# First stage of batches 3 to 7 from input folded twice, in rounds of sixteen 24x24 tiles; the last batch's evictions mostly on ScalarE

## The chip, the cores and the metric

The kernel runs on one core of one Trainium2 chip. The metric is the device time of one execution in microseconds; the figure that counts is the median of the runs shown. The engines go by their short names in the profile: PE is TensorE (its weight loads are PEld), DVE is VectorE, ACT is ScalarE, POOL is GpSimd and SP is SyncE.

## What is computed

The input x has 8 batches of 3008 positions with 256 channels. Each batch is filtered along its positions in the frequency domain, and the result goes through a two-layer network with an exact GELU:

```python
X = np.fft.rfft(x, axis=1)
y = np.fft.irfft(X * (filt_r + 1j * filt_i)[None], n=x.shape[1], axis=1)
h = y.reshape(24064, 256) @ w_in            # 256 -> 2048
g = 0.5 * h * (1.0 + erf(h / sqrt(2)))
out = g @ w_out                             # 2048 -> 256, float32
```

## The kernel before, in words

**The transform as four stages of matmuls.** 3008 = 47 x 64. A batch is seen as 47 rows (n1) of 64 positions (h = 0 or 1, w = 0 to 31). Stage one (`s1`) is a transform of length 47 over n1. Because x is real, the output is needed for 24 frequencies only (K1 = 24), a cosine and a sine part each. Before it `fold` (L104) forms sum and difference of the halves h = 0 and h = 1 in bf16 on DVE (L109, L110): four calls c a batch, each of 4 values of w in two groups v, 111 partitions x 1024 elements. `s1` (L414, matmuls on L429) then issues eight matmuls in a call: 47 rows of x against a table of 64 columns, 512 columns wide, into four PSUM banks (one of tag "h", three of tag "f"). Two banks are emptied by DVE (L327) and two by ACT (L325), and SP writes the result to a DRAM buffer R1 (L438). `r1` (L444, SP) reads R1 back as `b_sb`, in three parts u. `s2` (L456) is stage two, 32 small matmuls a burst; `s2_out` (L467, DVE) multiplies by the filter, `s2_sum` (L473, L474, DVE) adds up complex products, `s3` (L487) is stage three, `s3_out` writes to a DRAM buffer R2 (L497, SP), `r2` (L505, SP) reads it as `d_sb`, and `s4` (L514) is stage four, evicted into a ring `y_sb` of two batches of positions. Batch 0 goes another way (`c1` to `c4`) in the first 41 us.

**The network.** The 24064 positions form 47 token tiles t of 512. `mm1` (L640) makes 16 blocks jc of h in PSUM (tag "h", 3 banks), and ACT applies GELU (L643) into `g_sb`. The second layer of tile t-1 runs while tile t goes through the first. From t = 3 on it is `mm2_seven` (L698): seven products of half-size blocks take the place of eight, 112 matmuls of 128 columns (L714), with sums on DVE before (`sums_1` L685, `sums_2` L691, `sums_3` L696) and after (L729 to L743). Product m has matmuls 16m to 16m+15. They go through two PSUM banks of tag "o": product 0 in one, 1 and 2 in the other, 3 and 4 in the first, 5 and 6 in the second. Product 2 reads what `sums_2` writes, its second half (matmul 36 on) what the second L691 writes. L743 empties product 6, and `put_rows` (L761) writes the output rows, mostly from POOL.

**Order.** Every engine runs its instructions in the order in which they are recorded, and that order is laid out by hand in slots. A slot is one jc of one tile (slot = 16t + jc, about 0.83 us): whatever is put in the slot, then seven matmuls of `mm2_seven`, then one block of `mm1`. Batch b's stages are put in slots counted back from hi, the slot in which its first token tile begins (L918 to L945). Bursts of `s1` for batches 3 to 6 stand at hi-94, -91, -87 and -83, for batch 7 four slots earlier, and folds 20, 13, 8 and 6 slots ahead of hi-94. The x buffer is single: `load_next` (L144) loads the next batch's x in the slots of this batch's stage two, each time behind a small `gate` instruction on POOL that waits for a product of that stage. `table_4_factors` (L389) and `table_4_all` (L402, POOL) make the table of stage four in slots 46, 47, 89 and 105.

Of the kernel before, what the change touches and what calls it, by code (L numbers as in the profile page):

```python
# [18 lines left out]
NA, NB = 47, 64  # L19
# [12 lines left out]
class _Mix:  # L32
    def __init__(self, ctx, tc, x, filt_r, filt_i, w_in, w_out, out):
# [30 lines left out]
        self.s4_sb = f[:, 0:2048].bitcast(FP16).rearrange("p (i n) -> p i n", i=8)  # L64
        self.v_sb = [f[:, o:o + 1024].rearrange("p (c d) -> p c d", c=2) for o in (2048, 3072)]
        self.T4a = f[0:96, 4096:7168].rearrange("p (w m) -> p w m", w=HB)
        self.w_in_sb = c.tile([128, 2, self.DFF], BF16, name="w_in_sb")
# [15 lines left out]
    def load_x(self, lo=0, n=32, hs=(0, 1)):  # L83
        nc = self.nc
        if lo == 0 and 0 in hs:
            xt = self.px.tile([128, HB, 256], BF16, tag="x", name="x_sb")
            self.st[0, "x"], self.st["x1"] = xt[0:2 * NA], xt.rearrange("p (h w) c -> p h w c", h=2)
        xt, o = self.st[0, "x"], NA
        xv = self.x[0].rearrange("(n1 h w) d -> h n1 w d", h=2, w=HB)
        for w in range(lo, lo + n, 8):  # L90
            for h in hs:
                nc.gpsimd.dma_start(out=xt[h * o:h * o + NA, w:w + 8, :], in_=xv[h][:, w:w + 8, :])  # L92

    def load_x_pairs(self, b, c, h, n=1):
# [3 lines left out]
        for v in range(2):  # L98
            for to, at, m in ((0, 23, 24), (24, 0, 23)) if h else ((0, 0, NA),):
                w = 16 * v + 4 * c  # L100
                self.nc.gpsimd.dma_start(out=xt[64 * v + to:64 * v + to + m, h, 4 * c:4 * c + 4 * n, :],  # L101
                                         in_=xv[h][at:at + m, w:w + 4 * n, :])

    def fold(self, b, c):  # L104
# [39 lines left out]
    def load_next(self, b, p, c, h):  # L144
# [3 lines left out]
        else:  # L148
            self.gate(self.st[b, "p", p][0:1, p % 2, 1, 0, 0:1])
        self.load_x_pairs(b + 1, c, h)  # L150

# [180 lines left out]
    def table_1_tiles(self, g):  # L332
# [4 lines left out]
        for p in (0, 64):  # L337
            for r in (0, K1):
                v.tensor_copy(out=self.T1s[p:p + NA, r:r + K1].rearrange("p (u c m) -> p u c m", c=4, m=2),
                              in_=self.T1[0:NA, r:r + K1].rearrange("p (c u m) -> p u c m", u=3, m=2))  # L340

    def table_2_parities(self):

# [156 lines left out]
    def r2(self, b, c):  # L500
        d = self.pd.tile([96, 8, 256], BF16, tag="d", name="d_sb")
        self.st[b, "d", c] = d
        R2 = self.st[b, "R2"].rearrange("(r w) u a k m c -> r (u a k m) w c", r=2)
        for r in range(2):
            self.nc.sync.dma_start(out=d[r * 48:r * 48 + 48, :, :], in_=R2[r][:, 8 * c:8 * c + 8, :])  # L505

# [191 lines left out]
    def mm2_seven(self, t, lo, hi):  # L698
# [9 lines left out]
        for n in range(lo, hi):  # L708
# [32 lines left out]
            else:  # L741
                for h, tt, p in ((1, t3, p0), (0, t1, p1)):
                    v(out=c(h, 1 - h), in0=tt, in1=p, op=ALU.add)  # L743
                    for sub in range(2):
                        self.put_rows(t * TCH + 256 * h + 128 * sub, self.st["c"][h][:, sub],
                                      nc.gpsimd if t > 1 or h * sub == 0 else nc.sync)

# [35 lines left out]
def kernel(  # L783
# [135 lines left out]
    for b in range(1, B):  # L919
# [5 lines left out]
        for c in range(4):  # L925
            slot = (4, 8, 11, 13)[c] if b == 1 else s1 + int(c * n1)
            put((0, 1, 5, 8)[c] if b == 1 else (70, 74, 86, 94)[c] if b == 2 else hi - 94 - (20, 13, 8, 6)[c], m.fold, b, c)
            put(slot, m.s1, b, c)
# [11 lines left out]
        after[b] = s3 + 4  # L940
        crowd.update(range(s2[0], after[b]), range(s1 + 66, s1 + 94))
        if b + 1 < B:
            for i, (u, o, p) in enumerate(((0, 5, 1), (0, 7, 1), (1, 1, 2), (1, 5, 3), (1, 7, 3), (2, 1, 4), (2, 5, 5), (2, 7, 5))):
# [29 lines left out]
    put(9, m.table_4_rows, g)  # L973
    put(9, m.weights_4, g)
    put(23, m.table_u)
    put(46, m.table_4_factors, g)
    parts = [(w, h) for w in range(0, HB, 8) for h in range(2)]
    put(47, m.table_4_all, parts[:5])
    for slot, i, n in ((89, 5, 2), (105, 7, 1)):
        put(slot, lambda: m.gate(m.s4_sb[0:1, 7, 255:256]))  # L980
        put(slot, m.table_4_all, parts[i:i + n])
# [58 lines left out]
```

## Time and profile before

| | us |
|---|---|
| median of the 3 runs | 733.25 (733.07 to 733.67) |
| the profiled execution | 733.37 |
| its span in the profile | 731.6 |
| PE busy, all first-stage matmuls (L429) of 7 batches in the chain | 2.1% of the span |
| DVE busy | 595.1 |
| ACT busy | 576.6 |
| POOL busy | 283.9 |

The profile shows one execution. Its span goes from the first to the last instruction; the execution's own time is 1.77 us longer. Matmuls are pipelined, so their ends are modelled and a busy PE can still have waited: distances between starts tell more. "Idle before" of a group counts only what its own engine stood still. The engines' shares, by stretch of the span (busy us and instructions of each engine, granted clock, DMA share, GB/s), are even from batch 3 on:

```profile
core 0: us, PE busy (x) PEld busy (x) DVE busy (x) ACT busy (x) POOL busy (x), PEclk, DMA share, GB/s
...
354.00:443.00 89.00, 88.97 (x1195) 64.42 (x1193) 75.74 (x138) 71.89 (x132) 32.65 (x63) 1.00 0.50 125
443.00:532.00 89.00, 88.95 (x1155) 60.95 (x1153) 76.00 (x139) 71.84 (x132) 33.29 (x66) 1.00 0.51 126
532.00:621.00 89.00, 89.00 (x1218) 62.96 (x1216) 77.31 (x143) 73.05 (x136) 18.99 (x34) 1.00 0.42 118
```

Each of these stretches holds about one batch: 89 us, PE busy throughout at the full clock (1.00), DVE 76 us, ACT 72 us, and the 16 DMA engines half busy.

### The profile page before, as it was taken

How to read it: one execution, taken by the hardware profiler on the slowest of the kernel's cores; microseconds unless marked ns; L12 is line 12 of the kernel's file. 1: busy time of each engine (PE TensorE's matmuls, PEld its weight loads, DVE VectorE, ACT ScalarE, POOL GpSimd, SP SyncE). 2: the span in 40 equal slices, each digit the busy share in tenths (PEclk: the TensorE clock that was granted, in tenths of full speed). 3: DMA queues.
4: the chain of work that ended last, by engine and by line, in shares of the span. 5: the costliest groups of instructions: out<-in, count | busy, mean ns of one | idle time of the engine just before them, and what ended most of it. 6: DMA issues, size and time to landing. Idle time of an engine off the chain costs nothing.

```text
span 731.6 us, 22218 instructions
## 1 busy us (share of the span) xinstructions
PE 722.6 (99%) x9165; PEld 505.9 (69%) x9165; DVE 595.1 (81%) x1091; ACT 576.6 (79%) x1050; POOL 283.9 (39%) x545
## 2 busy tenths in 40 slices
PE   7999999999999999999999999999999999999997
PEld 4856675776777666676777667666677767777776
DVE  8985788899878998798976999779988897775666
ACT  7997778788877888778887788877888788877773
POOL 7944947364223462135511364115531121121121
PEclk9999999999999999999999999999999999999999
DMA  9886545664365553636535455355545443311011
GB/s 155 163 182 152 132 107 123 205 127 98 88 179 135 119 115 107 183 92 137 128 109 157 120 129 126 87 149 151 110 102 138 139 119 87 109 46 43 30 59 59
DMA packets 81254, 87.72 MB, mean 120 GB/s; under 512 B 13393, under 2 KB 61137, under 8 KB 81153
## 3 DMA queue, kind: packets, MB, share of 16 engines
q0 software_dynamic: 22288, 39.50, 24.1%
q1 hardware_dynamic: 58449, 46.62, 23.6%
q8 instruction: 71, 1.16, 0.7%
q14 instruction: 30, 0.25, 0.1%
q10 hardware_dynamic: 416, 0.20, 0.1%
HBM read 54.00 MB, written 46.66 MB: 138 GB/s over the span
## 4 chain that ended last, share of the span: by engine, by line
PE 94%; ACT 3%; DVE 1%; POOL 1%; DMA 1%; issue 0%; ACTq 0%; DVEq 0%; POOLq 0%
PE ps_h L640 44%; PE ps_o L714 38%; PE ps_o L656 3%; PE ps_s L514 3%; PE ps_s L429 2%; PE ps_s L456 2%; PE ps_s L487 2%; DMA F<-in_filt_i_dram 1%; ACT y_sb L325 1%; POOL x_sb L92 1%; ACT g_sb L643 1%; ACT vt_sb L325 0%; ACT b_sb L325 0%; PE ps_c L587 0%; DVE p L474 0%
## 5 line engine op out<-in xcount | busy, mean ns | idle before, releaser
L643 ACT ACTIVATE g_sb<-ps_h 128x512 f16<-128x512 f32 x752 | 446.3, 601 | 139.1 <-PE ps_h L640 130.4
L640 PE MATMUL ps_h<-y_sb,w_in_sb 128*128 128x512 bf16 (+3 forms) x1600 | 446.0, 366 | 0.3 <-ACT g_sb L643 0.3
L761 POOL DMA_DIRECT2D out_dram<-ost x231 | 131.8, 577 | 379.4 <-DVE ost L743 366.1
L714 PEld LDWEIGHTS <-g_sb 128*128 128x128 f16 x2816 | 184.4, 98 | 80.8 <-issue 14.6
L640 PEld LDWEIGHTS <-w_in_sb 128*128 128x128 bf16 x1600 | 126.2, 98 | 7.6 <-issue 1.6
L714 PE MATMUL ps_o<-w_sums,g_sb 128*128 128x128 f16 x1408 | 121.7, 219 | 0.3 <-DVE g_sb L691 0.2
L714 PE MATMUL ps_o<-w_sums,s_sb 128*128 128x128 f16 x1408 | 121.2, 219 | 0.0
L714 PEld LDWEIGHTS <-s_sb 128*128 128x128 f16 x1408 | 95.1, 98 | 37.6 <-issue 2.5
L685 DVE TENSOR_TENSOR s_sb<-g_sb 128x1024 f16<-128x1024 f16 x176 | 115.2, 685 | 0.7 <-ACT g_sb L643 0.6
L714 PE MATMUL ps_o<-w_out_sb,g_sb 128*128 128x128 f16 x1408 | 113.7, 219 | 0.0
L467 DVE TENSOR_TENSOR p<-ps_s,Fu 128x1024 bf16<-128x1024 f32 x84 | 101.5, 1217 | 9.1 <-PE ps_s L456 7.5
L101 POOL DMA_DIRECT2D x_sb<-in_x_dram x156 | 79.5, 516 | 2.8 <-issue 1.7
L691 DVE TENSOR_TENSOR g_sb<-s_sb,g_sb 128x1024 f16<-128x1024 f16 x88 | 60.4, 687 | 1.5
L714 PE MATMUL ps_o<-w_out_sb,F 128*128 128x128 f16 x704 | 60.6, 219 | 0.0
L696 DVE TENSOR_TENSOR F<-g_sb 128x1024 f16<-128x1024 f16 x88 | 60.0, 682 | 0.0
L714 PEld LDWEIGHTS <-F 128*128 128x128 f16 x704 | 47.1, 98 | 14.6 <-issue 0.4
L736 DVE TENSOR_TENSOR t_sb<-t_sb,ps_o 128x256 f32<-128x256 f32 x44 | 18.4, 417 | 40.4 <-PE ps_o L714 39.9
L514 PEld LDWEIGHTS <-d_sb 96*128 96x128 bf16 x448 | 31.3, 97 | 27.0 <-issue 1.7
L325 ACT ACTIVATE F<-ps_s 128x512 bf16<-128x512 f32 x83 | 45.5, 607 | 0.5 <-PE ps_s L487 0.4
L325 ACT ACTIVATE y_sb<-ps_s 128x376 bf16<-128x376 f32 x95 | 45.4, 478 | 0.1
L327 DVE CAST a_sb<-ps_s 128x512 bf16<-128x512 f32 x54 | 34.7, 684 | 12.0 <-PE ps_s L429 11.7
L743 DVE TENSOR_TENSOR ost<-t_sb,ps_o 128x256 f32<-128x256 f32 x86 | 32.1, 414 | 14.2 <-PE ps_o L714 14.2
(160 smaller groups left out, 588.7 us busy)
## 6 DMA issues: line engine op xcount, KB each, us to landing
out_dram<-ost POOLq DMA_DIRECT2D x127, 128.0 KB, 2.9
b_sb<-R SPq DMA_DIRECT2D x21, 512.0 KB, 4.9
R<-F SPq DMA_DIRECT2D x84, 128.0 KB, 2.4
d_sb<-R SPq DMA_DIRECT2D x56, 192.0 KB, 4.3
R<-a_sb SPq DMA_DIRECT2D x108, 96.0 KB, 2.2
x_sb<-in_x_dram POOLq DMA_DIRECT2D x48, 94.0 KB, 2.7
x_sb<-in_x_dram POOLq DMA_DIRECT2D x48, 48.0 KB, 2.7
x_sb<-in_x_dram POOLq DMA_DIRECT2D x12, 188.0 KB, 4.7
```

The source lines that it names most:

```text
L101: self.nc.gpsimd.dma_start(out=xt[64 * v + to:64 * v + to + m, h, 4 * c:4 * c + 4 * n, :], in_=xv[h][at:at + m, w:w + 4 * n, :])
L325: self.nc.scalar.activation(out=out, in_=in_, func=AF.Copy, scale=1.0 if scale is None else scale)
L327: self.nc.vector.tensor_copy(out=out, in_=in_)
L467: v(out=w[:, a], in0=ps.unsqueeze(2).to_broadcast([128, 2, 2, 256]), in1=f.unsqueeze(1).to_broadcast([128, 2, 2, 256]), op=ALU.mult)
L514: nc.tensor.matmul(ps[:, 94 * i:94 * i + 94], lhsT=d[:, (grp % 2) * 4 + i, 128 * half:128 * half + 128], rhs=self.T4a[:, 4 * grp + i, 0:2 ...
L640: nc.tensor.matmul(ps[:, o:o + n], lhsT=w[:, dc], rhs=self.ring[:, dc, off:off + n], start=(dc == 0), stop=(dc == 1))
L643: nc.scalar.activation(out=self.st["g", t][:, jc, :], in_=ps, func=AF.Gelu)
L685: self.nc.vector.tensor_tensor(out=self.st["s", t][:, i:i + 2], in0=a, in1=b, op=ALU.subtract)
L691: self.nc.vector.tensor_tensor(out=a21[:, k], in0=self.st["s", t][:, k, 0], in1=a22[:, k], op=ALU.add)
L696: self.nc.vector.tensor_tensor(out=self.s4_sb[:, k], in0=a12[:, k], in1=s2[:, k], op=ALU.subtract)
L714: nc.tensor.matmul(ps[:, (m + 1) % 2, sub, :], lhsT=a[:, i, 128 * sub:128 * sub + 128], rhs=b[:, i], start=i == 0, stop=i == 7)
L761: eng.dma_start(out=out, in_=tile_[lo - r0:lo - r0 + n])
```

## The change

For batches 3 to 7 the input is folded a second time. A cosine is even and a sine odd in n1, so rows n1 and 47-n1 can be added and subtracted ahead of stage one. That leaves 24 rows instead of 47 for each part. For this the rows 24 to 46 have to stand on the partitions of rows 23 to 1. `turn_x` (three POOL DMAs a batch, from DRAM to DRAM) writes the mirrored half of x as bf16 into a DRAM buffer xr, 12 slots ahead of the previous batch's stage two. `load_x_mirror` then loads the direct half from x (POOL) and the mirrored half from xr (SP), eight times each. `fold_mirror` runs eight DVE operations a batch on 120 partitions x 2048 elements: for each half k of w two from x into a scratch area in the F tile, then two back into x. Each stage-one call (`s1_mirror`) issues 16 matmuls of 24 rows x 32 columns, 512 columns wide, on 16 different tiles of the array (four row groups, each with a PSUM bank of its own, times four column groups). In batches 3 to 6 two of the four banks are emptied by DVE and two by ACT as before, in batch 7 one by DVE and three by ACT. The table T1m for it is made on POOL in slot 9.

Besides this, `table_4_factors` moves from slot 46 to 33 and five parts of `table_4_all` from slot 47 to slots 34, 51 and 53; the first `r2` of batch 6 is split in two halves of w; and the output rows of the last three tiles are written from SP instead of POOL.

```diff
@@ -63,6 +63,7 @@
         f = self.F.rearrange("p t k c -> p (t k c)")
         self.s4_sb = f[:, 0:2048].bitcast(FP16).rearrange("p (i n) -> p i n", i=8)
         self.v_sb = [f[:, o:o + 1024].rearrange("p (c d) -> p c d", c=2) for o in (2048, 3072)]
+        self.fold_t = f[:, 8192:12288].rearrange("p (d e w c) -> p d e w c", d=2, e=2, w=4)
         self.T4a = f[0:96, 4096:7168].rearrange("p (w m) -> p w m", w=HB)
         self.w_in_sb = c.tile([128, 2, self.DFF], BF16, name="w_in_sb")
         self.w_out_sb = c.tile([128, 16, self.D], FP16, name="w_out_sb")
@@ -84,7 +85,9 @@
         nc = self.nc
         if lo == 0 and 0 in hs:
             xt = self.px.tile([128, HB, 256], BF16, tag="x", name="x_sb")
+            self.px_x = xt
             self.st[0, "x"], self.st["x1"] = xt[0:2 * NA], xt.rearrange("p (h w) c -> p h w c", h=2)
+            self.st["xm"] = xt.rearrange("p (h e w) c -> p h e w c", h=2, e=2)
         xt, o = self.st[0, "x"], NA
         xv = self.x[0].rearrange("(n1 h w) d -> h n1 w d", h=2, w=HB)
         for w in range(lo, lo + n, 8):
@@ -100,6 +103,52 @@
                 w = 16 * v + 4 * c
                 self.nc.gpsimd.dma_start(out=xt[64 * v + to:64 * v + to + m, h, 4 * c:4 * c + 4 * n, :],
                                          in_=xv[h][at:at + m, w:w + 4 * n, :])
+
+    def turn_x(self, b):
+
+        D, n = self.D, NB * self.D
+        xr = self.st["xr"] = self.dram.tile([2, K1, HB, D], BF16, tag="xr", name="xr")
+        for h, to, at, m in ((0, 0, 0, 1), (0, 1, 46, 23), (1, 0, 23, 24)):
+            src = _dram(self.x, b * self.S * D + at * n + HB * h * D, [[2 * D, 16], [-n, m], [1, 2 * D]])
+            self.nc.gpsimd.dma_start(out=xr[h, to:to + m].rearrange("p (i w) c -> i p (w c)", w=2), in_=src)
+
+    def load_x_mirror(self, b, q, h):
+
+        D, n, p = self.D, NB * self.D, slice(32 * q, 32 * q + K1)
+        to = [self.st["xm"][p, h, e].rearrange("p (i e) c -> p i (e c)", e=2) for e in range(2)]
+        src = _dram(self.x, b * self.S * D + 23 * h * n + (HB * h + 2 * q) * D, [[n, K1], [8 * D, 4], [1, 2 * D]])
+        self.nc.gpsimd.dma_start(out=to[0], in_=src)
+        src = self.st["xr"][h].rearrange("p (i q e) c -> q p i (e c)", i=4, e=2)[q]
+        self.nc.sync.dma_start(out=to[1], in_=src)
+
+    def fold_mirror(self, b, k, i):
+
+        x, t, n = self.st["xm"][:, :, :, 4 * k:4 * k + 4], self.fold_t, 96 + K1
+        op = ALU.subtract if i % 2 else ALU.add
+        o, a0, a1 = (t[0:n, i], x[0:n, 0], x[0:n, 1]) if i < 2 else (x[0:n, :, i - 2], t[0:n, :, 0], t[0:n, :, 1])
+        self.nc.vector.tensor_tensor(out=o, in0=a0, in1=a1, op=op)
+
+    def s1_mirror(self, b, i):
+
+        nc, x = self.nc, self.st["xm"]
+        if i == 0:
+            self.st[b, "R1"] = self.dram.tile([NB, 48, 256], BF16, tag="R1", name="R1")
+        at = self.pa.tile([128, 8, 256], BF16, tag="a", name="a_sb")
+        ps = [self.bank("ps_s1", "f" if q else "h") for q in range(4)]
+        for d in range(2):
+            for t in range(2):
+                for q in range(4):
+                    p, o = slice(32 * q, 32 * q + K1), 64 * d + 32 * t
+                    nc.tensor.matmul(ps[q][o:o + 32, :], lhsT=self.T1m[p, t], rhs=x[p, d, t, 2 * i:2 * i + 2, :],
+                                     start=True, stop=True)
+        for q in range(4):
+            self._evac(at[:, 2 * q:2 * q + 2, :].rearrange("p w c -> p (w c)"), ps[q],
+                       "act" if q % 2 or q and b == self.B - 1 else False)
+        for d in range(2):
+            for t in range(2):
+                o, w = 64 * d + 32 * t, HB * d + 8 * i
+                nc.sync.dma_start(out=self.st[b, "R1"].rearrange("n q c -> q n c")[K1 * t:K1 * t + K1, w:w + 8],
+                                  in_=at[o:o + K1])
 
     def fold(self, b, c):
 
@@ -147,7 +196,14 @@
             self.gate(self.st[b, "d", 0][0:1, 0, 0:1])
         else:
             self.gate(self.st[b, "p", p][0:1, p % 2, 1, 0, 0:1])
-        self.load_x_pairs(b + 1, c, h)
+        if b < 2:
+            self.load_x_pairs(b + 1, c, h)
+            return
+        if b == 2 and c == h == 0:
+            n = NB * self.D
+            self.nc.gpsimd.dma_start(out=self.px_x[94:96].rearrange("p w c -> p (w c)"),
+                                     in_=_dram(self.x, 0, [[n, 2], [1, HB * self.D]]))
+        self.load_x_mirror(b + 1, c, h)
 
     def load_w_in(self):
         wi = self.w_in.rearrange("(dc p) j -> p dc j", p=128)
@@ -338,6 +394,19 @@
             for r in (0, K1):
                 v.tensor_copy(out=self.T1s[p:p + NA, r:r + K1].rearrange("p (u c m) -> p u c m", c=4, m=2),
                               in_=self.T1[0:NA, r:r + K1].rearrange("p (c u m) -> p u c m", u=3, m=2))
+
+    def table_1_mirror(self, g):
+
+        v = self.nc.gpsimd
+        self.T1m, half = g.tile([128, 2, 32], BF16, name="T1m"), g.tile([128, 1], FP32, name="half")
+        v.memset(half, 1.0)
+        v.memset(half[0:1], 0.5)
+        v.memset(self.T1m, 0.0)
+        for p in range(0, 128, 32):
+            for r in range(2):
+                v.tensor_scalar(out=self.T1m[p:p + K1, r, 0:K1].rearrange("p (u c m) -> p u c m", c=4, m=2),
+                                in0=self.T1[0:K1, K1 * r:K1 * r + K1].rearrange("p (c u m) -> p u c m", u=3, m=2),
+                                scalar1=half[0:K1], scalar2=None, op0=ALU.mult)
 
     def table_2_parities(self):
 
@@ -501,8 +570,10 @@
         d = self.pd.tile([96, 8, 256], BF16, tag="d", name="d_sb")
         self.st[b, "d", c] = d
         R2 = self.st[b, "R2"].rearrange("(r w) u a k m c -> r (u a k m) w c", r=2)
-        for r in range(2):
-            self.nc.sync.dma_start(out=d[r * 48:r * 48 + 48, :, :], in_=R2[r][:, 8 * c:8 * c + 8, :])
+        n = 4 if c == 0 and b == self.B - 2 else 8
+        for w in range(0, 8, n):
+            for r in range(2):
+                self.nc.sync.dma_start(out=d[r * 48:r * 48 + 48, w:w + n, :], in_=R2[r][:, 8 * c + w:8 * c + w + n, :])
 
 
     def s4(self, b, grp, half, eng):
@@ -743,7 +814,7 @@
                     v(out=c(h, 1 - h), in0=tt, in1=p, op=ALU.add)
                     for sub in range(2):
                         self.put_rows(t * TCH + 256 * h + 128 * sub, self.st["c"][h][:, sub],
-                                      nc.gpsimd if t > 1 or h * sub == 0 else nc.sync)
+                                      nc.gpsimd if self.B * self.S // TCH - 3 > t > 1 or h * sub == 0 and t < 2 else nc.sync)
 
     def put_rows(self, r0, tile_, eng):
 
@@ -924,6 +995,11 @@
         busy.update(range(s1 - 1, s1 + int(3 * n1) + 2))
         for c in range(4):
             slot = (4, 8, 11, 13)[c] if b == 1 else s1 + int(c * n1)
+            if b > 2:
+                for i in range(2):
+                    put(s1 - e // 2 - (15, 13, 11, 9, 6, 3, 0, -3)[2 * c + i], m.fold_mirror, b, c // 2, c % 2 * 2 + i)
+                put(slot, m.s1_mirror, b, c)
+                continue
             put((0, 1, 5, 8)[c] if b == 1 else (70, 74, 86, 94)[c] if b == 2 else hi - 94 - (20, 13, 8, 6)[c], m.fold, b, c)
             put(slot, m.s1, b, c)
         for u in range(3):
@@ -939,6 +1015,8 @@
             busy.update(range(s2[u] - 1, s2[u] + 5), range(s3 - 1, s3 + 2))
         after[b] = s3 + 4
         crowd.update(range(s2[0], after[b]), range(s1 + 66, s1 + 94))
+        if 1 < b < B - 1:
+            put(s2[0] - 12, m.turn_x, b + 1)
         if b + 1 < B:
             for i, (u, o, p) in enumerate(((0, 5, 1), (0, 7, 1), (1, 1, 2), (1, 5, 3), (1, 7, 3), (2, 1, 4), (2, 5, 5), (2, 7, 5))):
                 put((76, 77, 80, 81)[i - 4] if b == 1 and i > 3 else s2[u] + o, m.load_next, b, p, i // 2, i % 2)
@@ -972,12 +1050,13 @@
     put(9, m.table_u_pick, g)
     put(9, m.table_4_rows, g)
     put(9, m.weights_4, g)
+    put(9, m.table_1_mirror, g)
     put(23, m.table_u)
-    put(46, m.table_4_factors, g)
+    put(33, m.table_4_factors, g)
     parts = [(w, h) for w in range(0, HB, 8) for h in range(2)]
-    put(47, m.table_4_all, parts[:5])
-    for slot, i, n in ((89, 5, 2), (105, 7, 1)):
-        put(slot, lambda: m.gate(m.s4_sb[0:1, 7, 255:256]))
+    for slot, i, n in ((34, 0, 1), (51, 1, 2), (53, 3, 2), (89, 5, 2), (105, 7, 1)):
+        if slot > 88:
+            put(slot, lambda: m.gate(m.s4_sb[0:1, 7, 255:256]))
         put(slot, m.table_4_all, parts[i:i + n])
     put(18, m.move_filters, 2, 4)
     put(20, m.weight_sums)
```

## The prediction, made before the changed kernel was run

> **What bounds the kernel now.** I read the page first: busy shares, then the chain of work that ended last.
>
> ```profile
> PE 722.6 (99%) x9165; PEld 505.9 (69%) x9165; DVE 595.1 (81%) x1091; ACT 576.6 (79%) x1050; POOL 283.9 (39%) x545
> ...
> PE 94%; ACT 3%; DVE 1%; POOL 1%; DMA 1%; issue 0%; ACTq 0%; DVEq 0%; POOLq 0%
> ```
>
> TensorE is the bound. A busy PE can hide waits, so I also took the distance from each matmul's start to the next in the trace's records. From 42 us to 721 us only one gap between full-size matmuls is over 0.3 us (0.37, at 110 us). So whatever leaves TensorE's stream there comes off the time, provided no other engine is late instead. One first-stage burst, in the timeline of PE (start, length, instruction):
>
> ```profile
> 376.57 0.40 PE L429 MATMUL ps_s<-xs,T1s 47*64 47x512 bf16 x2
> 376.58 0.40 PE L429 MATMUL ps_s<-x_sb,T1s 47*64 47x512 bf16 x2
> 376.81 0.38 PE L429 MATMUL ps_s<-xs,T1s 47*64 47x512 bf16 x2
> 376.82 0.38 PE L429 MATMUL ps_s<-x_sb,T1s 47*64 47x512 bf16 x2
> 377.13 0.29 PE L714 MATMUL ps_o<-w_out_sb,g_sb 128*128 128x128 f16 x2
> ```
>
> Eight matmuls go as two rounds of four, side by side, 0.24 us apart; the next full-size matmul starts 0.31 us after the second round. The burst holds the stream for 0.56 us.
>
> **TensorE's gain.** s1_mirror puts 16 matmuls, each again of 512 columns, into one round on 16 tiles. In s2's bursts (L456) the records show eight tiles of a round starting 3.4 ns apart, so 16 take 0.05 us. First start to next full-size matmul: 0.05 + 0.31 = 0.36 us; saved 0.56 - 0.36 = 0.20 us. Five batches of four bursts: 20 x 0.20 = **4.0 us**. The trace has no round of 16. Its nearest rows run eight: s2's 2 x 4 tiles and s3's 4 x 2, both at full rate. Bounds: 4.0 us saved if 16 run at once, nothing if eight do (two rounds), 9.6 us lost if four do (two rounds of 0.24 us more, 20 times). I take 4.0, as s2 shows four streams in one row group and s3 four row groups.
>
> **What VectorE pays.** Per batch the old fold is eight operations on 1024 elements; the new one is eight on 2048. The groups (mean ns after the comma):
>
> ```profile
> L685 DVE TENSOR_TENSOR s_sb<-g_sb 128x1024 f16<-128x1024 f16 x176 | 115.2, 685 | 0.7 <-ACT g_sb L643 0.6
> L110 DVE TENSOR_TENSOR x_sb<-x_sb 111x1024 bf16<-111x1024 bf16 x28 | 19.4, 692 | 1.0
> L473 DVE TENSOR_TENSOR p<-p 128x512 bf16<-128x512 bf16 x42 | 18.5, 441 | 0.0
> L671 DVE TENSOR_TENSOR w_sums<-w_out_sb 128x1024 f16<-128x1024 f16 x2 | 1.7, 833 | 0.0
> ```
>
> Queued back to back, starts lie 0.60 us apart at 1024 elements (timeline below) and 0.335 at 512, so 0.53 us per 1024: a fold of 2048 takes 0.60 + 0.53 = **1.13 us** of the queue. L671, whose runs are 128 elements long, is the slowest such row: 0.78 us apart, 1.55 us at 2048. I take 1.13, since the fold's runs are 1024 long as in L110. An old pair took 0.72 + 0.61 = 1.33 us (the second waits for the first). Per batch 8 x 1.13 - 4 x 1.33 = +3.7 us on an engine that is off the path. What counts is who is queued behind.
>
> *Batches 3 to 6* (folds 15 slots before the first burst to 3 after; a slot is about 0.83 us). I walked batch 5's queue with these distances. Copy L729 starts at 363.2 as before; two folds and an L696 put L731 at 366.4 (366.1 now); two folds later DVE has caught up, since L736 waits for PE until 370.2. Then a fold, two L685, a fold and the rest: the second L691 starts at 377.4 (376.5 now; its reader comes at 380), the first eviction at 378.0 (377.1 now). The second ends at 379.3, and the next burst takes that bank at 379.5. The last fold ends at 383.0; the third burst, which reads it, is due at 383.3. So it fits, with 0.1 to 0.2 us over; in batch 4 the same walk comes out 0.1 us short. I take +0.1 us.
>
> *Batch 7* (folds two slots later relative to its bursts). Before:
>
> ```profile
> 538.85 0.68 DVE L691 TENSOR_TENSOR g_sb<-s_sb,g_sb 128x1024 f16<-128x1024 f16 x1
> 539.45 0.68 DVE L685 TENSOR_TENSOR s_sb<-g_sb 128x1024 f16<-128x1024 f16 x1
> 540.17 0.69 DVE L691 TENSOR_TENSOR g_sb<-s_sb,g_sb 128x1024 f16<-128x1024 f16 x1
> ```
> ```profile
> 542.14 0.33 PE L714 MATMUL ps_o<-w_sums,g_sb 128*128 128x128 f16 x3
> ```
>
> The second L691 writes what the second of these matmuls reads, at 542.20. DVE is busy without a gap from 535.06 to there. Ahead of that L691 the change takes out one old pair and queues three folds: 540.17 - 1.33 + 3.39 = 542.23, plus its 0.69 = 542.92, plus 0.06 that a waiting matmul starts later. PE waits **0.8 us**. Walking on, the two L743 of the next tile end 1.1 us later than now, while their bank is wanted only 0.4 later (0.8 of wait, less two bursts' 0.2 each); now they end at 554.15 with the bank's next matmul at 554.12, so the first of the two seems to be enough, and I take **0.45 us** (0.8 if both count). The move of evictions to ScalarE is in this sum: without it two more 0.61 us stood in front by then. It costs ACT 0.48 us a burst. Its gelus come 0.83 us apart and take 0.50 of its queue, so it is covered; if it were not, 4 x 0.48 = 1.9 us.
>
> **Loads.** POOL issues 24 loads of 0.5 us for a batch now; then 8, and turn_x's 3, whose larger descriptor lists no row shows (from 0.5 us, as L101, to a few us). POOL is idle 61% of the time and behind turn_x wait gates and rows of output: nothing. SP gets 8 more issues of 0.4 us, behind which R's and b_sb's transfers stand; xr is due 17 slots, 14 us, after its turn, while a load of x lands in 4.7 us at most. Nothing, unless xr is late. The first fold now needs all loads; the last was issued at 354.8 and lands in 3 us, the fold is due at 363.5.
>
> The transfers themselves collide. turn_x moves about 750 packets of 1 KB; the packets of 2 KB of x take 215 ns each, so by half of that 750 x 0.108 / 16 = 5 us of all 16 DMA engines. For batch 3 it runs from 128 us, just when batch 2's R1 is written and read back:
>
> ```profile
> 134.84 0.81 SPq L444 DMA_DIRECT2D b_sb<-R  x2
> ...
> DMA to landing us min/median/max: 3.5/4.3/4.8
> ```
>
> The first lands at 138.3; s2 reads it at 139.3. One microsecond is free, and DMA is 70 to 100% busy there. Bounds: nothing to 3 us. In batches 3 to 6 there are 4 to 7 us free. I take +0.4 us, near the lower end, as 2.4 us of the 7 before 135 us are idle.
>
> **At nothing:** the split first r2 (a wait that PE does not show), earlier table_4_factors and table_4_all on an idle POOL (15 us uncovered at worst, but first used 25 slots later), T1m (2 us of POOL at slot 9), and the last three tiles' rows on SP: the end is set by the stores issued at 728.1 and 728.4, after POOL's drain ended at 727.96.
>
> **A rule against it.** After s2's burst of 32 matmuls at 573.12, the first eviction starts at 573.67; the modelled end of the 16 matmuls that it needs is 573.52, so it follows by 0.15 us. The Trainium skill, "TensorE: Matmul & The Clock Gate", section "The cost: per-tile semaphore tail", says that 16 tiles that each signal add 25 + 4.7 x 16 + 26.3 x 16 = 521 ns. By it evictions would start some 0.4 us later, and as an estimate each of 20 bursts could lose up to that, 8 us, the gain gone twice. The trace's 0.15 does not bear it out.
>
> **Sum.** -4.0 + 0.1 + 0.8 + 0.45 + 0.4 = -2.25 us. The profiled execution took 733.37 (span 731.6): 731.1. The median of the runs, 733.25, is 0.12 lower: **731.0 us**.
>
> **Rivals.**
> - *All is hidden:* folds a little shorter or batch 7's waits taken up elsewhere: 733.25 - 4.0 = 729.3. For it: such waits are worked out to tenths. Against: batch 7's queue has no gap. 0.20.
> - *The turn collides:* 2 to 3 us more at s2 of batch 2 (and 3): 733 to 734. 0.10.
> - *The tiles do not run 16 at once* (the change does not do what it says): no gain, 1.75 lost: 735.0. 0.05.
> - *VectorE becomes the bound*, the other side: each of 40 folds over 1.13 us delays sums and evictions with no margin left behind them. From 1.13 + 2.25/40 = 1.19 us it can eat the gain; at L671's 1.55 it costs up to 40 x 0.42 = 17 us: 748. Against it speaks the length of the runs; for it the margins of 0.1 us. 0.10.
> - *The forecast:* 0.55, its own range 729.8 to 732.0.
>
> About 0.2% (1.5 us) is what a measurement can tell from no change, so faster means below 731.8. Forecast (nearly all of it) and the first rival are faster: 0.73; the collision and the forecast's edge are the same: 0.12; the last two rivals are slower: 0.15. The range takes in all but these two: 729.0 to 734.0.
>
> **What would show it.** Bursts of 16 at 0.36 us from first start to next full-size matmul; folds starting 1.13 us apart; TensorE waiting 0.8 us for an L691 ahead of batch 7's first burst, and for L743 after the second; s2 of batch 2 waiting for b_sb at most 1 us. Wrong: a burst still at 0.56, folds above 1.2, waits for DVE in every batch, or s2 waiting for DMA.

## The result

The changed kernel is slower by 0.6%: **737.77 us** (median of 6, 735.62 to 738.91) against 733.41 for the kernel before on the same chip (6, 732.89 to 733.74). The ratio is 1.0057, 95% interval 1.0040 to 1.0073. The forecast was 731.0, and the range ended at 734.0.

In the changed kernel the lines have moved: L685, L691, L743 and L714 of before are L756, L762, L814 and L785; `mm1` is L711, `s4`'s matmul L585, `r2` L576, `turn_x` L113, `fold_mirror` L129, `s1_mirror` L142. The profiled execution took 738.66 us, its span 736.9. The page's busy times and its chain:

```profile
PE 714.1 (97%) x9174; PEld 507.5 (69%) x9325; DVE 610.8 (83%) x1087; ACT 577.2 (78%) x1054; POOL 251.8 (34%) x484
...
PE 80%; DMA 5%; DVE 5%; POOL 4%; issue 3%; ACT 2%; SPq 0%; DVEq 0%; POOLq 0%
```

PE is busy for 8.5 us less, and yet the span is 5.3 longer: TensorE now stands and waits. The chain has DMA at 5% instead of 1%, DVE at 5% instead of 1%. Where that happens shows when the start of every matmul of the second layer is compared in both traces, the n-th with the n-th:

| place | us |
|---|---|
| slot 108 (tile 5): from `s4` of batch 1 on | +7.67 |
| 20 bursts of stage one, 0.16 to 0.19 each | -3.77 |
| batch 4: `mm1` waits for its bank after the third burst | +0.19 |
| batch 7: L814 late for matmul 16 of tile 33 | +0.15 |
| batch 7: L762 late for matmul 36 of tile 33 | +0.64 |
| two waits of 0.06 (tiles 28 and 34), one old wait gone (tile 27, -0.17) | -0.05 |
| start, up to tile 3 | +0.48 |
| sum (the profiled executions differ by 5.29) | +5.31 |

The start differs from run to run (from 0.0 to 0.5 us in the runs below, 0.9 in e8), so it is not counted as the change's. Nor is the old wait at tile 27: it is missing in all other traces, in e3 and e10 too, where folds and bursts are as before, so it belongs to the one profiled execution of the kernel before. All else is small beside one place. There the timeline of PE reads (start, length, instruction; in brackets how long the engine stood and for whom):

```profile
134.62 0.60 PE L711 MATMUL ps_h<-y_sb,w_in_sb 128*128 128x512 bf16 x2
139.89 0.49 PE L585 MATMUL ps_s<-F,d_sb 96*128 96x94 bf16 x4 [4.67 <-DMA d_sb<-R]
140.18 0.95 PE L785 MATMUL ps_o<-w_sums,g_sb 128*128 128x128 f16 x7
```

TensorE stands 4.67 us for `d_sb`, which `r2` of batch 1 reads back from DRAM. SP issued these reads at 128.99 and 129.83, among the three issues of `turn_x` on POOL (128.37 to 130.18):

```profile
128.37 1.81 POOL L113 DMA_DIRECT2D xr<-in_x_dram  x3
...
128.99 1.36 SPq L576 DMA_DIRECT2D d_sb<-R  x2
```

Seven matmuls then take 0.95 us instead of 0.55. The table of stretches says why (columns: stretch and its length, then busy us of PE, PEld, DVE, ACT and POOL, then the granted clock, DMA share, GB/s; a packet's whole time counts in the stretch in which it starts, so a share can exceed 1). First two stretches of the kernel before, then four of the kernel after:

```profile
130.00:134.00 4.00, 4.00 (x47) 2.82 (x45) 1.62 (x4) 2.87 (x6) 2.20 (x4) 1.00 0.76 216
134.00:138.00 4.00, 4.00 (x55) 3.06 (x53) 3.08 (x7) 3.13 (x6) 0.53 (x1) 1.00 0.54 163
```

```profile
130.00:134.00 4.00, 4.00 (x46) 2.84 (x45) 2.10 (x5) 2.87 (x6) 1.93 (x4) 1.00 0.99 169
134.00:138.00 4.00, 1.17 (x10) 0.59 (x9) 1.17 (x3) 1.40 (x3) 0.98 (x1) 1.00 1.13 224
138.00:142.00 4.00, 2.11 (x16) 1.56 (x17) 1.58 (x3) 0.00 (x0) 0.00 (x0) 0.62 0.16 43
142.00:146.00 4.00, 4.00 (x32) 2.90 (x31) 0.32 (x2) 2.04 (x4) 0.00 (x0) 0.52 0.97 319
```

From 130 to 138 us all DMA engines are busy (0.99 and 1.13; before, 0.76 and 0.54). Then the clock is granted at half speed, from 138.99 to 145.81 us, 6.8 us long. So the 7.67 us are 4.95 of delay at the wait and 2.72 lost at the half clock after it. The transfers of the turn landed at 132.41, 136.63 and 139.66; their 768 packets of 1 KB took 111 ns each on average, 768 x 0.111 / 16 = 5.3 us of all engines.

This is the profiled execution. The mean granted clock is on record for all six: 0.994 to 0.995 in three of them (737.81, 738.66 and 738.91 us), 0.997 to 0.998 in the other three (735.62, 736.36 and 737.73 us). By the same arithmetic (6.8 us at half in 737 take 0.0046 off the mean, 3.4 us take 0.0023), the half clock lasted about 3.4 us in the latter; this is an estimate.

The gain itself came. A burst of 16 and what follows it, in batch 7:

```profile
556.36 0.43 PE L142 MATMUL ps_s<-x_sb,T1m 24*32 24x512 bf16 x16
556.72 0.56 PE L785 MATMUL ps_o<-w_out_sb,F 128*128 128x128 f16 x7
```

0.37 us from first start to the next full-size matmul (0.366 to 0.369 in 18 of the 20 bursts, 0.39 in the other two). And the wait in batch 7, first DVE's queue, then PE:

```profile
545.02 0.68 DVE L762 TENSOR_TENSOR g_sb<-s_sb,g_sb 128x1024 f16<-128x1024 f16 x1
545.62 1.21 DVE L129 TENSOR_TENSOR x_sb<-F 120x2048 bf16<-120x2048 bf16 x1
546.76 0.68 DVE L756 TENSOR_TENSOR s_sb<-g_sb 128x1024 f16<-128x1024 f16 x1
547.47 0.69 DVE L762 TENSOR_TENSOR g_sb<-s_sb,g_sb 128x1024 f16<-128x1024 f16 x1
```
```profile
547.52 0.22 PE L785 MATMUL ps_o<-w_sums,g_sb 128*128 128x128 f16 x1
548.22 0.51 PE L785 MATMUL ps_o<-w_sums,g_sb 128*128 128x128 f16 x6 [0.48 <-DVE g_sb L762]
```

A fold holds the queue for 1.14 us (545.62 to 546.76), and the second L762 ends at 548.16, just ahead of the matmul at 548.22 that reads it.

### The profile page after: what moved, and what is told of

The parts are those of the page before. It is cut to its first block, busy times and chain, and to the rows that moved or that the text cites. A ratio compares the mean times of both kernels' runs of the same rounds, so it can differ in the third digit from the quotient of the medians.

```text
span 736.9 us, 22361 instructions
## 1 busy us (share of the span) xinstructions
PE 714.1 (97%) x9174; PEld 507.5 (69%) x9325; DVE 610.8 (83%) x1087; ACT 577.2 (78%) x1054; POOL 251.8 (34%) x484
## 4 chain that ended last, share of the span: by engine, by line
PE 80%; DMA 5%; DVE 5%; POOL 4%; issue 3%; ACT 2%; SPq 0%; DVEq 0%; POOLq 0%
PE ps_o L785 37%; PE ps_h L711 35%; PE ps_s L585 3%; DMA x_sb<-in_x_dram 3%; PE ps_s L525 1%; PE ps_s L556 1%; ACT g_sb L714 1%; DMA d_sb<-R 1%; PE ps_o L727 1%; PE ps_s L142 1%; POOL F L186 1%; DVE s_sb L756 1%; DMA F<-in_filt_i_dram 1%; POOL T2p L417 1%; DVE a_sb L383 1%
## 5 line engine op out<-in xcount | busy, mean ns | idle before, releaser
L714 ACT ACTIVATE g_sb<-ps_h 128x512 f16<-128x512 f32 x752 | 445.6, 602 | 143.1 <-PE ps_h L711 119.9
L711 PE MATMUL ps_h<-y_sb,w_in_sb 128*128 128x512 bf16 (+3 forms) x1453 | 416.2, 366 | 0.7 <-ACT g_sb L714 0.3
L832 POOL DMA_DIRECT2D out_dram<-ost x223 | 126.5, 574 | 382.9 <-DVE ost L814 366.2
L785 PEld LDWEIGHTS <-g_sb 128*128 128x128 f16 x2816 | 184.8, 98 | 79.1 <-issue 12.0
L711 PEld LDWEIGHTS <-w_in_sb 128*128 128x128 bf16 x1600 | 126.6, 98 | 7.8 <-issue 1.6
L785 PE MATMUL ps_o<-w_sums,g_sb 128*128 128x128 f16 x1408 | 122.7, 220 | 2.1 <-DVE g_sb L762 0.7
L785 PE MATMUL ps_o<-w_sums,s_sb 128*128 128x128 f16 x1408 | 121.3, 219 | 1.7
L785 PEld LDWEIGHTS <-s_sb 128*128 128x128 f16 x1408 | 95.1, 98 | 36.8 <-issue 1.5
L756 DVE TENSOR_TENSOR s_sb<-g_sb 128x1024 f16<-128x1024 f16 x176 | 114.9, 683 | 1.0 <-ACT g_sb L714 0.6
L785 PE MATMUL ps_o<-w_out_sb,g_sb 128*128 128x128 f16 x1408 | 113.9, 220 | 1.8
L785 PE MATMUL ps_o<-w_out_sb,F 128*128 128x128 f16 x704 | 61.3, 221 | 1.0
L762 DVE TENSOR_TENSOR g_sb<-s_sb,g_sb 128x1024 f16<-128x1024 f16 x88 | 60.4, 687 | 1.5
L785 PEld LDWEIGHTS <-F 128*128 128x128 f16 x704 | 47.6, 98 | 14.8 <-issue 0.8
L585 PEld LDWEIGHTS <-d_sb 96*128 96x128 bf16 x448 | 31.8, 98 | 32.3 <-DMA d_sb<-R 5.2
L814 DVE TENSOR_TENSOR ost<-t_sb,ps_o 128x256 f32<-128x256 f32 x86 | 32.2, 415 | 18.2 <-PE ps_o L785 18.2
L585 PE MATMUL ps_s<-F,d_sb 96*128 96x94 bf16 x448 | 37.7, 207 | 5.6 <-DMA d_sb<-R 4.7
L802 DVE TENSOR_TENSOR ost<-t_sb,ps_o 128x256 f32<-128x256 f32 x44 | 18.2, 414 | 23.1 <-PE ps_o L785 23.1
```

The source lines that it names most:

```text
L585: nc.tensor.matmul(ps[:, 94 * i:94 * i + 94], lhsT=d[:, (grp % 2) * 4 + i, 128 * half:128 * half + 128], rhs=self.T4a[:, 4 * grp + i, 0:2 ...
L711: nc.tensor.matmul(ps[:, o:o + n], lhsT=w[:, dc], rhs=self.ring[:, dc, off:off + n], start=(dc == 0), stop=(dc == 1))
L714: nc.scalar.activation(out=self.st["g", t][:, jc, :], in_=ps, func=AF.Gelu)
L756: self.nc.vector.tensor_tensor(out=self.st["s", t][:, i:i + 2], in0=a, in1=b, op=ALU.subtract)
L762: self.nc.vector.tensor_tensor(out=a21[:, k], in0=self.st["s", t][:, k, 0], in1=a22[:, k], op=ALU.add)
L785: nc.tensor.matmul(ps[:, (m + 1) % 2, sub, :], lhsT=a[:, i, 128 * sub:128 * sub + 128], rhs=b[:, i], start=i == 0, stop=i == 7)
```

## The experiments

**Theory:** the turn of batch 3 takes the DMA engines from the reads of `d_sb`; TensorE's stand then brings the half clock. All else is as forecast. **Rivals:** the double fold on VectorE is what costs; or the stand is only seen there and the time would be lost elsewhere anyway. Times are medians; each group of four ran on one chip with the kernel before (733.29, 733.28 and 733.16 us for e1 to e4, e5 to e8 and e9 to e12). Of longer edits only the lines that matter are shown. Delays in the text are taken from the starts of matmuls; the views of waits count only the time that an engine stood, which is a little less.

### The turn later (e1)

```diff
-            put(s2[0] - 12, m.turn_x, b + 1)
+            put(s2[0] - 12 + 16 * (b == 2), m.turn_x, b + 1)
```

> The changed kernel with batch 3's turn_x 16 slots later (slot 117 in place of 101), nothing else. Theory: in slot 101 its 10 us of transfers delay batch 1's d_sb, TensorE waits 4.8 us for it in slot 108 and then runs at half clock to 145.8 us; the token tiles show 7.67 us lost there. Without it: 737.8 - 7.7 = 730.1, tile 6 of the trace about 0.5 us behind the kernel before in place of 8.15, clock 1.0 from then on. Rival: d_sb is late for another reason (the moved table work, the SP queue): about 737.8 and the same gap. Second rival: the collision only moves to batch 2's second stage or to the x loads, which then show a DMA wait of their own: 732 to 736.

Measured: **730.82** (730.77 to 730.96), ratio 0.9963 (0.9950 to 0.9976). The same stretches:

```profile
134.00:138.00 4.00, 4.00 (x53) 3.06 (x52) 2.85 (x7) 2.95 (x6) 0.76 (x1) 1.00 0.50 131
138.00:142.00 4.00, 4.00 (x73) 2.66 (x70) 3.96 (x8) 2.26 (x5) 2.24 (x4) 1.00 1.03 303
142.00:146.00 4.00, 4.00 (x48) 2.84 (x46) 4.00 (x6) 3.10 (x6) 2.98 (x6) 1.00 0.83 225
```

PE is busy throughout at 1.00, and no wait for a DMA is left there. By putting three transfers 16 slots later, about 7 us are regained, and the change is a gain of 2.5. The spread shrinks from 3.3 us to 0.2. The theory holds; VectorE's part is as small as the table says.

### The clock apart from the wait (e2)

The kernel after, with 23 matmuls of 128x512 on constants, whose results nobody reads, ahead of slot 108 (the function that issues them is left out; lines from there on are 5 higher, so `s4` is L590):

```diff
+    at[108].insert(0, (m.keep_busy, (23,)))
```

> The changed kernel with 23 idle matmuls of 128x512 (0.216 us each, 5.0 us) put in front of the fourth-stage matmuls of slot 108, whose results nobody reads; nothing is left out. They fill the wait for d_sb and so keep the array busy. Theory: of the 7.67 us lost, about 4.9 are the wait and the rest is the half clock after it; the wait is now filled and the clock stays at 1.0: 2.8 us less than the changed kernel in the same run, about 735.0. Rival: the half clock is not caused by the idle time: it comes all the same, about 737.8 or more.

Measured: **736.53** (735.74 to 738.23), ratio 1.0043 (1.0028 to 1.0057). Timeline of PE, and one stretch:

```profile
135.01 5.13 PE L381 MATMUL ps_busy<-ones 128*128 128x512 bf16 x23
140.16 0.34 PE L590 MATMUL ps_s<-F,d_sb 96*128 96x94 bf16 x4
```
```profile
138.00:142.00 4.00, 3.98 (x36) 2.28 (x35) 1.47 (x3) 0.64 (x2) 0.00 (x0) 1.00 0.19 51
```

`s4` starts as late as in the kernel after (140.16 against 139.89), but with no stand the clock stays at 1.00. The mean clock is 0.999 to 1.000 in all five executions, and no transfer was changed. So the half clock comes from TensorE standing, not from the transfers. The time is 1.5 us above what was expected. From tile 3 on the trace gains 2.08 us on that of the kernel after: the 2.72 of the half clock, less 0.40 for `s2` of batch 2, which now waits for `b_sb`, since TensorE comes to it sooner, and less 0.20 by which `s4` is later here (5.15 of delay against 4.95), and 0.04 in small steps. The rest of the 1.5 us is in what the expectation started from, a median of executions that differ by 3.3 us. Here they still differ by 2.5 us at full clock, so the half clock is not the whole of that spread.

### The transfers alone (e3)

The kernel before with `turn_x` of batch 3 in the slot in which the kernel after has it. It writes xr, which nobody reads (the function itself, as in the change, is left out here).

```diff
+        if b == 2:
+            put(s2[0] - 12, m.turn_x, b + 1)
```

> The kernel before with batch 3's turn_x added in slot 101 as in the change; nothing reads its buffer, all else is as before. Theory: these three transfers alone make d_sb late: tile 6 comes 7 to 8 us later than before, 741 (740 to 742). Rival: it takes the change's other transfers or the moved table work too: 733.4.

Measured: **740.31** (739.25 to 741.08), ratio 1.0091 (1.0075 to 1.0107). From the waits (engine, line, releaser: us in total, times, longest):

```profile
PE ps_s L522 <- DMA d_sb<-R: 4.2, 1, 4.2
```

L522 is this kernel's `s4`. The delay there is 4.44 us, and the clock is half from 139.01 to 142.43, which costs 1.48 more. No fold and no burst differs from before here: the three transfers are the whole cause. As a median it is 7.0 us slower than before, as expected.

### Half the turn (e7)

The kernel after; of batch 3's turn the third transfer, 384 of 768 packets, goes 16 slots later (what `turn_x` does with the numbers is left out; lines are 2 higher).

```diff
+            put(s2[0] - 12, m.turn_x, b + 1, (0, 1) if b == 2 else (0, 1, 2))
+            if b == 2:
+                put(s2[0] + 4, m.turn_x, b + 1, (2,))
```

> The kernel after, of batch 3's turn only the third transfer (384 of 768 packets of 1 KB) moved sixteen slots later; the first two stay. Theory (packets take the 16 DMA engines' time: 768 of 111 ns are 5.3 us, 384 are 2.7): d_sb's wait of 4.95 us in slot 108 falls by 2.7, to about 2.3 us, and as TensorE then stands too short for the half clock, the 2.7 us of that go whole: 738.7 - 2.7 - 2.7 = 733.3 us. Rival (what counts is that the reads stand in line behind the turn at all, not how much it moves): the wait stays at 4 to 5 us and the half clock with it, 737 to 738. Second rival (a threshold: the queue takes 2.7 us without anybody waiting): no wait, 730.8.

Measured: **735.31** (732.95 to 736.11), ratio 1.0016 (1.0004 to 1.0028).

```profile
134.66 0.59 PE L713 MATMUL ps_h<-y_sb,w_in_sb 128*128 128x512 bf16 x2
138.06 0.34 PE L587 MATMUL ps_s<-F,d_sb 96*128 96x94 bf16 x4 [2.80 <-DMA d_sb<-R]
138.23 0.56 PE L787 MATMUL ps_o<-w_sums,g_sb 128*128 128x128 f16 x7
138.63 0.87 PE L713 MATMUL ps_h<-y_sb,w_in_sb 128*128 128x512 bf16 x2
```

The delay falls from 4.95 to 2.97 us, by 2.0 where half of the packets' time is 2.7. So the amount counts, as the theory has it. What I had wrong is the clock: a stand of 2.8 us can be enough. It is granted at half from 138.8 on, when TensorE already works again, for 3.4 us, and costs 1.65. Of the ten times, four lie at 732.95 to 733.82 and six at 735.19 to 736.11. The mean granted clock on record is 0.999 to 1.000 in the lower four, as in the kernel before, and 0.997 to 0.998 in the upper six. So the expectation of 733.3 without the half clock came true in four executions of ten, and the half clock came in six. Only one of the six was profiled, so how long TensorE stood in the four is not shown.

### Batch 7's third fold a slot later (e4), and the last one too (e5)

e4 is e1 with the third fold one slot later, e5 is e4 with the last one, too:

```diff
-                    put(s1 - e // 2 - (15, 13, 11, 9, 6, 3, 0, -3)[2 * c + i], m.fold_mirror, b, c // 2, c % 2 * 2 + i)
+                    put(s1 - e // 2 - (15, 13, 11 - e // 4, 9, 6, 3, 0, -3)[2 * c + i], m.fold_mirror, b, c // 2, c % 2 * 2 + i)
```
```diff
-                    put(s1 - e // 2 - (15, 13, 11 - e // 4, 9, 6, 3, 0, -3)[2 * c + i], m.fold_mirror, b, c // 2, c % 2 * 2 + i)
+                    put(s1 - e // 2 - (15, 13, 11 - e // 4, 9, 6, 3, 0, -3 - e // 4)[2 * c + i], m.fold_mirror, b, c // 2, c % 2 * 2 + i)
```

> As e1, and batch 7's third fold one slot later (546 in place of 545), which puts it behind the second sums_2 (L762). Theory: the 0.64 us that TensorE waited for that L762 at 547.5 us goes, and nothing else is late: 0.6 us under e1, about 729.5. Rival: the fold only delays what comes next (copy, fourth fold, the first burst), so the same 0.6 us is lost a little later.

> The kernel after with the turn of batch 3 sixteen slots later, batch 7's third fold one slot later (as in the run before) and its last fold one slot later, too. Theory (batch 7's waits are VectorE's queue: a fold of 1.2 us that stands in front of what TensorE waits for): the wait of 0.44 us for L814 at matmul 16 of tile 34 goes, since the last fold is what stands in front of it, and nothing else comes late: 730.0 us, 0.4 under the run before. Rival (no room left in the queue; a wait only moves): the same 730.4, with a new wait of about 0.4 us a little later in tile 34 or 35, for L762 or for the fourth burst, which reads what the last fold writes.

Measured: e4 **730.45** (730.25 to 730.56), ratio 0.9957 (0.9941 to 0.9974); e5 **730.76** (730.36 to 731.07), ratio 0.9963 (0.9949 to 0.9977). The waits from 549 to 556 us, of e4 and then of e5:

```profile
PE ps_o L785 <- DVE ost L814: 0.3, 1, 0.3
```
```profile
PE ps_h L711 <- DVE a_sb L383: 0.4, 1, 0.4
```

In e4 the 0.64 us for L762 are gone, but L814 now comes 0.44 late for matmul 16 of tile 34. Apart from the start, e4's trace gains 2.96 us on before where e1's gains 2.78: 0.2 of the 0.6 that were expected, so the rival was right in the main. In e5 that wait is gone, and `mm1` waits 0.53 for its bank at matmul 28 instead; its trace gains 2.99 us, no more than e4's. The rival was right here too, though it had named another reader: in a full queue a moved fold only moves the wait.

### Which evictions go to ScalarE in batch 7 (e6, e9, e12, e11)

e6 is e5 with two of four on ScalarE, as in the other batches. e9 is e5 with three of four, but so that VectorE keeps the second bank and ScalarE takes the first, the "h" bank that `mm1` waits for. e12 is e9 with the last fold back in its slot. e11 is e9 with banks 1 and 3 on ScalarE in batches 3 to 6. The lines with + are those of e6, of e9 and e12, and of e11. The expectations of e11 and e12 mean e9 by the first kernel, that of e6 means e5 by the run above.

```diff
-                       "act" if q % 2 or q and b == self.B - 1 else False)
+                       "act" if q % 2 else False)
+                       "act" if (q != 1 if b == self.B - 1 else q % 2) else False)
+                       "act" if (q != 1 if b == self.B - 1 else q % 2 == 0) else False)
```

> The kernel of the run above with two instead of three of four evictions on ScalarE in the last batch. It tells what that part of the change is worth. Forecast's reason: two evictions of 0.61 us more stand in VectorE's queue by the time of the second wait, so 0.4 to 1.2 us more: 730.4 to 731.2, with a wait for VectorE in batch 7 in the trace. Rival (the part does nothing, since by now the folds stand where there is room): within 0.2 us of the run above, no wait for VectorE above 0.2 us.

> The kernel with batch 7's last fold one slot later, and there in the last batch ScalarE empties the first bank of a burst (tag h, which mm1 waits for) and VectorE the second (tag f). Theory (the 0.5 us at matmul 28 of tile 34 are mm1 waiting for the h bank, whose eviction stands behind folds on VectorE; ScalarE's queue is short): that wait goes, nothing new above 0.2 us: 0.4 to 0.5 us under 730.76, so 730.3. Rival (VectorE is simply full there, whatever it is given comes late, and what waits next is a sum or the f bank): the same total, 730.7, with a wait for VectorE at another matmul.

> As the first kernel of this call, but the last fold of batch 7 back in its slot. Theory (the last fold stands in front of L814, whatever the evictions do): the 0.44 us at matmul 16 of tile 34 stay, nothing at matmul 28: 730.4. Rival (the eviction of the h bank stood in that queue as well, and a bank less to wait for makes room): 730.0.

> As the first kernel of this call, and in batches 3 to 6, too, ScalarE empties banks 1 and 3 of a burst (the h bank among them) and VectorE banks 2 and 4. Theory: the 0.19 us in batch 4, where mm1 waits for the h bank after the third burst, go, and nothing else changes: 0.2 us under the first kernel. Rival (an f bank, now emptied last by VectorE, comes late for the next burst or for stage two): 0.2 to 1 us over it, with a wait of s1 or s2 for VectorE.

Measured: e6 **731.55** (731.32 to 732.39), ratio 0.9975 (0.9965 to 0.9984). The same stretch of its waits:

```profile
PE ps_h L711 <- DVE a_sb L383: 1.0, 1, 1.0
```

The wait of `mm1` at matmul 28 is 1.13 us here instead of 0.53. So three evictions instead of two on ScalarE are worth 0.76 us in the trace, as the forecast reasoned. e9: **729.94** (729.86 to 730.04), ratio 0.9951 (0.9938 to 0.9963), the fastest of all; the 0.53 us are gone, and no wait for VectorE over 0.2 us is left in batch 7. e12: 730.46 (729.97 to 730.67), ratio 0.9957 (0.9945 to 0.9970); the 0.44 us of e4 are back at matmul 16, as expected. e11: 730.01 (729.69 to 730.25), ratio 0.9951 (0.9939 to 0.9964); in its trace batch 4's 0.19 is gone, 0.12 come in at tile 9, and its net gain is 3.57 us against e9's 3.38, but its start took 0.34 longer, so the times cannot tell the two apart.

### The small parts (e8), and all turns alone (e10)

e8 is e5 with the tables of stage four back in slots 46 and 47, `r2` of batch 6 in one piece, and the last three tiles' rows on POOL. e10 is the kernel before with all five turns, batch 3's 16 slots later, used by nobody. The diffs are e8's part for the rows, and e10's slots for `turn_x`. The expectation of e8 means e5 by the first kernel.

```diff
-                                      nc.gpsimd if self.B * self.S // TCH - 3 > t > 1 or h * sub == 0 and t < 2 else nc.sync)
+                                      nc.gpsimd if t > 1 or h * sub == 0 else nc.sync)
```
```diff
+        if 1 < b < B - 1:
+            put(s2[0] - 12 + 16 * (b == 2), m.turn_x, b + 1)
```

> The first kernel of this call without the three small parts that were put at nothing: the tables of stage four back in slots 46 and 47, the first r2 of batch 6 in one piece, the rows of the last three tiles on GpSimd. Theory (all three are off the path): within 0.2 us of the first kernel. Rival (one of them pays: rows on GpSimd at the end, or table work beside T1m on GpSimd): 0.3 to 2 us slower, with a wait for GpSimd or a longer end in the trace.

> The kernel before with all five turns as well (batch 3's sixteen slots later), written to DRAM and used by nobody. Two questions. First, is there any cost of the turns apart from batch 3's place: theory no, so 733.3 to 733.6 from TensorE's stream. Second, what makes GpSimd's last drain longer (4.8 us before, 9.8 in the kernel after): if it is the turns, about 9.8 us here too, and since the last rows stand on GpSimd here, the end moves to 723.8 + 9.8 = 733.2 us in the span plus 0.8, so 736; if it is the new loads of x, 4.8 us and no change, 733.4.

Measured: e8 **733.78** (733.19 to 734.34), ratio 1.0006 (0.9997 to 1.0015), 3.0 above e5. TensorE's stream is the same: the distance to e5 is 0.47 us at tile 3 and 0.47 at the last matmul. The end is not. POOL's drains, e8 and then the kernel before (times, ns least/median/most, first and last start):

```profile
L1114 POOLq DRAIN  x3: 46/97/10473, 721.1 to 732.1; - x3
```
```profile
L1035 POOLq DRAIN  x3: 46/245/4762, 723.2 to 731.3; - x3
```

The drain behind the last rows on POOL takes 10.5 us instead of 4.8 and ends at 731.59, with the last instruction at 732.4. With the rows on SP it starts at 694.3 in e5 and is over by 704.1. So this part, put at nothing, keeps 2.9 us from coming up; the tables and `r2` do not show in TensorE's stream from tile 3 on. Whether the tables have a part in the 0.47 us ahead of it, one start among many that differ, is not shown. e10: 732.73 (732.23 to 733.74), ratio 0.9991 (0.9982 to 1.0000). The turns apart from batch 3's place cost nothing, and the drain took 5.98 us, neither the 9.8 nor the 4.8 that were expected. So the turns are a part of what makes it longer; whether the rest is the new loads of x was not separated.

## Why the prediction was wrong, point by point

**The step that failed** is "The transfers themselves collide": "I take +0.4 us, near the lower end, as 2.4 us of the 7 before 135 us are idle", with bounds "nothing to 3 us". It measured 7.67. The 5 us for the turn's packets was right (5.3). Wrong was whom they hit, and what it costs when TensorE stands:

- I looked at one reader, `s2` of batch 2 with `b_sb`. The reads of `d_sb` of batch 1 stand on SP in the same microseconds. In before the first of these landed at 132.96 and its matmul came at 134.57, 1.6 us later (when the second landed is not in the trace). e3 shows that these transfers alone delay it by 4.44 us.
- The half clock was not priced at all. It adds 2.72 us in the profiled execution, and e2, without the stand, has none.
- The rival "The turn collides" had the right cause, the transfers, but the same reader and no half clock, and so, from the same bounds, 733 to 734 us.

**What held.** A burst at 0.37 us (0.36), 0.16 to 0.19 saved (forecast 0.20): 3.77 of 4.0. A fold at 1.13 to 1.14 us from start to start in 36 of 40 (1.13), 1.29 to 1.32 in four. Batches 3 to 6: 0.19 and 0.06 of new waits (forecast +0.1). The wait for the second L762 in batch 7: 0.64 (0.8), at the matmul that was named. With the collision away, e1 took 730.82; the forecast without its 0.4 is 730.6. That they are so near is partly luck: in e1's trace the bursts saved 0.2 less than forecast, and the waits, 1.1 us instead of 1.35, cost 0.2 less.

**L743 after the second burst, 0.45 us:** did not come in the kernel after. I took the bank's next matmul to be due at 554.12; matmul 16 of tile 34 starts at 554.96 in before, a slot later. In e4, where the first wait is gone and the matmul comes earlier by so much, 0.44 us appear just there. So the queue was rightly suspected; that the number is the forecast's is chance, as the forecast had the first wait in it.

**What was put at nothing:** the tables and the split `r2` cost nothing that shows from tile 3 on (e8), and ScalarE's extra evictions gain (e6). For the rows on SP I named the wrong reason: not that the stores set the end anyway, but that a longer drain, which the change brings, would have set it.

**The rule against it.** The 521 ns that the Trainium skill gives in "TensorE: Matmul & The Clock Gate", section "The cost: per-tile semaphore tail", are for 16 matmuls that each signal a semaphore. In the trace of the kernel after only four of the 16 matmuls of a burst do (nine in the last burst of batches 3 to 6), and two of the 32 in the burst of `s2` that the prediction held against the rule. So neither that 0.15 us nor this kernel tests the 521 ns; the prediction took the sentence for a case that it does not describe. What the trace shows: where the engine stood free, the first eviction starts 0.09 us after the modelled end of a burst with four signals (DVE, the last two bursts of batch 7) and 0.30 us after one with nine (ACT, four bursts). In the other 14 bursts the first eviction stands behind a GELU in ACT's queue and starts 0.14 to 0.21 us after that end.

**Rivals that fell:** folds above 1.19 us (1.22 in length, but 1.13 to 1.14 apart in 36 of 40), and tiles not running 16 at once.

## What to carry to other kernels

Before a transfer is added, list every read-back whose time in flight it overlaps, with its reader and its margin; a transfer of 5 us must find that much free behind each, or a place further off. A stand of the bounding engine for a few us is to be priced with the half clock after it. In a queue without gaps, moving one instruction moves the wait; what helps is giving work to another engine, and of several pieces the one that the bounding engine waits for.

## What the runs showed of the hardware

- After a stand of 2.8 to 4.7 us TensorE's clock was granted at half for 3.4 us (e3, e7) or 6.8 us (the kernel after). The traces' records of the clock show where this begins: in all three 133.12 us after the first rise to full clock (at 5.87 us of the span in the kernel after, 5.89 in e3, 5.69 in e7). That is 39 times 3413 ns, and the half clock lasts one or two such lengths. In the 14 traces of this case the first rise lies anywhere from 4.4 to 6.3 us. The Trainium skill, "TensorE: Matmul & The Clock Gate", section "What's actually happening", tells of free-running windows of 3413 ns, of which an idle one halves the clock. The lengths and the grid agree. That a whole window must be idle does not: in e7 the window from 135.40 to 138.81 has TensorE at work from 138.06 on, so 2.66 us of standing in it were enough.
- Why the half clock lasted two windows in the kernel after is not shown. TensorE stood 0.90 us of the window that began at 138.99 there, 0.07 us of the one at 139.01 in e3, and none of the one at 138.81 in e7.
- Packets of 1 KB that turn fp32 into bf16 from DRAM to DRAM took 111 ns each on average in the kernel after (768 of them), 117 in e10, and three transfers of them on POOL's queue delayed what waits for reads on SP's queue by 4.4 to 5.1 us (e3, the kernel after, e2).
- POOL's last drain took 4.8 us in before, 6.0 with five turns more, 9.8 to 10.5 in the kernels with the whole change, and it ran beside other work when the last rows left from SP.
